# Retention, then a Sinkhorn mixture of experts: X and w1 operands in small steps with moved loads, third tokens after six blocks of columns, Sinkhorn in smaller pieces

## The chip, the core and the metric

The kernel runs on one core of a Trainium2 chip. A time is the device time of one execution in microseconds; the time of a kernel is the median of its runs. The engines are named as in the profile: PE (TensorE), DVE (VectorE), ACT (ScalarE), POOL (GpSimd), SP (SyncE, which issues most DMAs).

## What is computed

```python
# retention: B, H, S, D = 4, 8, 768, 64
for t in range(S):
    state = gamma[None, :, None, None] * state + einsum('bhd,bhe->bhde', k[:, :, t], v[:, :, t])
    y[:, :, t] = scale * einsum('bhd,bhde->bhe', q[:, :, t], state)
x = y.transpose(0, 2, 1, 3).reshape(3072, 512)        # N tokens, D = 512
# mixture of experts: E = 8, F = 1024
P = exp(x @ w_gate - max)                             # (3072, 8)
for _ in range(8):
    P /= P.sum(1, keepdims=True) + 1e-09
    P /= P.sum(0, keepdims=True) + 1e-09
    P *= N / E
for e in range(E):
    out += P[:, e:e + 1] * (maximum(x @ w1[e], 0) @ w2[e])
```

All inputs and the output are float32.

## The kernel before

**Precision and products.** Every float32 operand of the large matmuls is split into a rounded high part (`hi_act`, line 76, on ACT) and the rest (`lo`, line 79: full minus high, on DVE or POOL). A product is then three matmuls: high x high, low x high, high x low. Both large matrix products use a 2 x 2 block scheme with seven products M1 to M7 in place of eight, so operands need sums of blocks ahead (M5, M6, M7, M4 of x; M5, M6, M3, M7 of w1), and results need sums behind.

**Attention stage** (lines 255 to 436). The sequence is cut into 24 chunks (6 places of 128 tokens for each of 4 batches), one chunk `gc` a step `tau` of the loop in line 412. A step decays k on POOL (`tk`), loads the chunk three ahead, splits q and k of the chunk two ahead (`split_qk`: ACT rounds, POOL makes `kl`, DVE makes `QL`), computes the scores of the next chunk (PE, then DVE writes `ta`), the logits of the chunk before, the attention of its own (PE, DVE writes `RX`, SP stores it to `xd` in DRAM) and the state update (PE, DVE adds). Steps 20 to 23 have no state update. SP's queue is in order: the loads of a step stand behind the store of the step before. At the end of step 8 (`tau == 2 * B`) SP is given the load of X0 (the first third of the tokens, in 8 DMAs of 256 KB) and of the w1 blocks 0 and 1 (512 KB each); from step 9 on two tasks of a list are run in each step: 22 for X0 (`x_tasks`), then 3 for each of the two w1 blocks (`w1_tasks`: four additions on POOL and the rounding on ACT, then two subtractions on DVE).

**First matrix product** (lines 707 to 764). A unit is one block of w1's columns (j, 32 of them) by one third of the tokens (r = 0, 1, 2): seven products of 6 matmuls of 128 x 128 x 512, 42 in all. Within a unit's row the products stand in the order `ROW` (M6, M1 of the next unit, M3, M7, M2 and M5 of the next, M4); after each come its results' sums (`post`, `sums`, `last_sum`, on ACT and DVE) and, at certain places m of the row, a task from the list `wq` (w1 blocks) or `xq` (X). Each engine runs its instructions in the order written here. X0 holds the first third, X1 the second; the third goes into X0 again. w1 blocks are converted in jobs, with three buffers `WA` and two raw buffers in `RW`. The list `order` (line 244) gives the units: units 0 to 31 are r = 0 over all 32 blocks; units 32 to 34 are r = 1 of blocks 29, 30, 31; units 35 to 37 are r = 2 of the same; then one block at a time with r = 1 and 2, and the last three blocks as a group. At unit 0 the X1 tasks begin (line 709; its loads stand ahead of the units in SP's queue, with w1 block 2 behind them, line 710); at unit 32 X0 is loaded with the third tokens and its tasks are queued, two after every product (lines 723 to 725, 747).

**Sinkhorn** (lines 450 to 506). The list `sink` has 19 pieces, run one at the end of each unit from 12 to 30: the maximum (DVE reduces, PE transposes, DVE reduces), the exponential (PE broadcasts, then 17 DVE instructions, with XSC as scratch, which the X tasks use too), 8 pairs of row and column steps, and a transposition of P.

**Second matrix product** (lines 533 to 770): units of the same kind over the experts and the three thirds. The change doesn't touch it.

## Time and profile before

| | |
|---|---|
| median of 3 runs | 2055.17 us (2054.22 to 2057.34) |
| profiled execution | 2053.89 us, span 2051.8 us |
| mean granted clock of PE | 0.987 |
| PE, DVE, ACT, POOL busy | 1985.9, 1527.7, 1041.7, 406.0 us |
| DMA | 504.13 MB, mean 246 GB/s |
| attention stage | to 166.3 us |
| first matrix product | 166.3 to 1136.3 us |
| second matrix product | 1136.3 us to the end |

The profile is one execution. Busy time is the sum of an engine's instructions; "idle" in a row is the time before an instruction in which its engine did nothing, with what ended that. The granted clock is the share of full speed that PE was given. A table of windows gives each engine's busy time in a stretch, so stages can be told apart. The chain of work that ended last is by line 42% `L190` (the first product's matmuls) and 25% and 19% `L551` (the second's).

### The profile page before, as it was taken

The page shows a single profiled execution, that of the slowest core. Times are in us where ns is not written, and L with a number is a line of the kernel's source. Part 1 is how long each engine was busy: PE and PEld are TensorE (multiplying, and loading weights), DVE is VectorE, ACT ScalarE, POOL GpSimd, SP SyncE. Part 2 cuts the span into 40 slices and gives each one's busy share as a digit, 9 for nine tenths or more (in the row PEclk, how much of TensorE's full clock was granted, in tenths as well). Part 3 has the DMA queues.
Part 4 walks back from the last instruction along what each step waited for, and adds up shares of the span by engine and source line. Part 5 has one row for each costly group of instructions (what it writes and reads, how often), then busy time and mean ns, then how long its engine had stood idle before and what let it go on. Part 6 is the DMA issues. An engine that isn't in the chain of part 4 may idle for free.

```text
span 2051.8 us, 28824 instructions
## 1 busy us (share of the span) xinstructions
PE 1985.9 (97%) x9273; PEld 1647.2 (80%) x9273; DVE 1527.7 (74%) x2083; ACT 1041.7 (51%) x1668; POOL 406.0 (20%) x422
## 2 busy tenths in 40 slices
PE   7797999998899999999999999999999999999998
PEld 7786887887688888888887788888888888888887
DVE  6795988995666666666677787878778777868766
ACT  3343564554444444444444565655555555655553
POOL 5462342341211121121123000100100101001001
PEclk9899999999999999999999999999999999999999
DMA  7755776776466666666667888998999999999997
GB/s 240 239 180 163 242 245 206 244 244 217 165 233 214 218 228 217 221 218 223 220 229 263 297 286 281 278 288 277 285 283 278 267 291 270 291 292 269 271 269 184
DMA packets 253191, 504.13 MB, mean 246 GB/s; under 512 B 27824, under 2 KB 40432, under 8 KB 250992
## 3 DMA queue, kind: packets, MB, share of 16 engines
q1 hardware_dynamic: 241088, 458.78, 66.3%
q0 software_dynamic: 11952, 43.52, 11.0%
q8 instruction: 72, 1.18, 0.2%
q14 instruction: 79, 0.65, 0.1%
HBM read 269.31 MB, written 232.88 MB: 245 GB/s over the span
## 4 chain that ended last, share of the span: by engine, by line
PE 90%; DVE 4%; DMA 3%; issue 1%; ACT 1%; SPq 1%; POOL 0%; DVEq 0%; ACTq 0%
PE psA L190 42%; PE psA L551 25%; PE psB L551 19%; DMA raw<-kT 1%; DVE QL L80 1%; PE ps_s L327 1%; PE ps_x L363 1%; DMA RW<-w 1%; PE psA L372 1%; PE ps_x L358 0%; PE ps_t L339 0%; DVE X L80 0%; DVE ta L330 0%; SPq L112 0%; DMA hd<-OT 0%
## 5 line engine op out<-in xcount | busy, mean ns | idle before, releaser
L190 PE MATMUL psA<-X,WA 128*128 128x512 f32 x4032 | 931.4, 393 | 24.1 <-DVE OT L213 18.8
L190 PEld LDWEIGHTS psA<-X,WA 128*128 128x128 f32 x4032 | 760.8, 189 | 190.2 <-DVE OT L213 20.9
L77 ACT ACTIVATE WA<-WA 128x512 fp32r<-128x512 f32 x668 | 403.1, 629 | 259.3 <-PE psB L551 116.7
L551 PE MATMUL psA<-WA,X 128*128 128x512 f32 x2296 | 531.4, 389 | 0.2 <-DVE XSC L562 0.2
L551 PEld LDWEIGHTS psA<-WA,X 128*128 128x128 f32 x2296 | 431.0, 188 | 89.9 <-issue 0.6
L551 PE MATMUL psB<-WA,X 128*128 128x512 f32 x1728 | 404.3, 390 | 5.1 <-ACT WA L77 3.1
L80 DVE TENSOR_TENSOR WA<-WA,WA 128x512 fp32r<-128x512 f32 x487 | 313.7, 685 | 99.4 <-ACT WA L77 94.9
L551 PEld LDWEIGHTS psB<-WA,X 128*128 128x128 f32 x1728 | 324.6, 188 | 74.8 <-ACT WA L77 4.2
L158 POOL TENSOR_TENSOR RW<-RW 128x256 f32<-128x256 f32 x244 | 220.8, 915 | 637.9 <-DMA RW<-w 412.8
L219 ACT ACTIVATE OT<-OT 128x512 f32<-128x512 f32 x96 | 60.7, 632 | 243.3 <-DVE OT L218 243.3
L80 DVE TENSOR_TENSOR WA<-RW,WA 128x768 fp32r<-128x768 f32 x122 | 142.5, 1169 | 54.0 <-ACT WA L77 53.9
L569 POOL DMA_DIRECT2D out<-XSC x56 | 48.5, 865 | 611.7 <-DVE XSC L564 365.6
L80 DVE TENSOR_TENSOR WA<-WA 128x512 fp32r<-128x512 f32 x181 | 121.7, 697 | 35.4 <-ACT WA L77 34.4
L213 DVE TENSOR_TENSOR OT<-psA,OT 128x512 f32<-128x512 f32 x96 | 66.2, 689 | 106.2 <-PE psA L190 106.2
L77 ACT ACTIVATE WA<-RW 128x768 fp32r<-128x768 f32 x122 | 109.4, 946 | 23.6 <-POOL RW L158 13.9
L225 DVE TENSOR_TENSOR OT<-psA,OT 128x512 f32<-128x512 f32 x96 | 66.2, 690 | 58.5 <-ACT OT L219 51.3
L229 ACT ACTIVATE OT<-psA 128x512 f32<-128x512 f32 x96 | 57.5, 599 | 77.1 <-PE psA L190 40.3
L236 DVE TENSOR_TENSOR OT<-OT 128x512 f32<-128x512 f32 x96 | 92.2, 961 | 3.3
L579 ACT ACTIVATE OT<-psA 128x512 f32<-128x512 f32 x96 | 57.4, 598 | 72.7 <-PE psA L551 68.8
L226 ACT ACTIVATE OT<-OT 128x512 f32<-128x512 f32 x96 | 60.7, 633 | 65.4 <-DVE OT L225 65.3
L240 DVE TENSOR_TENSOR OT<-OT 128x512 f32<-128x512 f32 x96 | 70.1, 730 | 30.0 <-ACT OT L229 26.1
L211 ACT ACTIVATE OT<-psA 128x512 f32<-128x512 f32 x96 | 57.4, 598 | 64.0 <-PE psA L190 63.9
(116 smaller groups left out, 1486.4 us busy)
## 6 DMA issues: line engine op xcount, KB each, us to landing
hd<-OT SPq DMA_DIRECT2D x672, 256.0 KB, 2.6
WA<-hd SPq DMA_DIRECT2D x668, 256.0 KB, 6.1
RW<-w SPq DMA_DIRECT2D x61, 512.0 KB, 4.5
out<-XSC POOLq DMA_DIRECT2D x56, 512.0 KB, 8.3
RW<-w SPq DMA_DIRECT2D x16, 1024.0 KB, 7.7
out<-OT POOLq DMA_DIRECT2D x27, 512.0 KB, 8.4
OT<-pd SPq DMA_DIRECT2D x23, 512.0 KB, 6.2
raw<-kT SPq DMA_DIRECT2D x24, 256.0 KB, 4.0
```

Source lines behind the costliest of these rows:

```text
L77: act.activation(o, i, AF.Copy)
L80: eng.tensor_tensor(o, full, rd(h), ALU.subtract)
L158: eng_add.tensor_tensor(x[:, WP[o]], x[:, WP[p]], x[:, WP[q]], op)
L190: pe.matmul(ps, w[:, a, k * P:(k + 1) * P], x[:, b, k * 512:(k + 1) * 512], start=i in PRE and k == 0 and m == 0, stop=k == 1 and m == 2, ...
L213: dve.tensor_tensor(c12, ps, u2, ALU.add)
L219: act.activation(o, o, AF.Relu)
L225: dve.tensor_tensor(o, ps, s1, ALU.add)
L226: act.activation(o, o, AF.Relu)
L229: act.activation(self.new("A12"), ps, AF.Relu)
L236: dve.tensor_tensor(t["S2"], t["S1"], t["A11"], ALU.subtract)
L240: dve.tensor_tensor(self.new("S4"), self.t["A12"], self.t["S2"], ALU.subtract)
L551: pe.matmul(ps[d] if isinstance(ps, tuple) else ps[:, d, :], w[:, a, q * 256 + d * P:q * 256 + d * P + P], h[b], start=i in PRE and q == 0 ...
```

## The change

Seven edits:
- `x_load` can load one half of a third of the tokens (one of its two places in the sequence) by itself; M2's loads come second. X0's first half (4 DMAs) is asked for at step 5, its second half at step 8, behind w1 blocks 0 and 1.
- w1 blocks 2 and 3 are loaded at step 16 of the attention stage. Before, block 2 came behind X1's loads and block 3 after unit 0.
- `x_tasks`: 22 steps as before, but the rounding on ACT is issued some steps ahead of the subtraction that reads it, and the sums of blocks stay on DVE.
- `w1_tasks` has four steps: the rounding on ACT is a step of its own. They are run after the products 0, 3, 5, 6 of a unit's row (before: three steps at 0, 1, 5).
- In the attention stage the w1 tasks come first, interleaved, from step 10 on; X0's tasks follow, two a step, and the last two after the logits.
- Order: units 32 to 37 are r = 1 of six blocks, 38 to 40 r = 2 of three of these, 41 to 43 r = 2 of the first three, for which w1 is converted again (64 jobs, before 61). X1's tasks begin at unit 1; the third tokens are loaded at unit 32, and their tasks run from unit 33 on, five a unit, every third subtraction on POOL.
- Sinkhorn has 23 pieces, from unit 14 on: the maximum in three, the exponential in three of six instructions; the transposition is at unit 38.

```diff
--- before.py
+++ after.py
@@ -106,16 +106,16 @@
             q.pop(0)()
 
 
-    def x_load(t, r):
-        for i, c, d in ((M1, 0, 0), (M7, 1, 0), (M3, 1, 1), (M2, 0, 1)):
-            for k in range(2):
+    def x_load(t, r, which=(0, 1)):
+        for i, c, d in ((M1, 0, 0), (M2, 0, 1), (M7, 1, 0), (M3, 1, 1)):
+            for k in range(2) if c in which else ():
                 sp.dma_start(rd(t[:, XP[i], 1, k * 512:(k + 1) * 512]).rearrange("p (b s) -> p b s", s=C),
                              xd[2 * r + c][:, :, 2 * d + k, :])
 
     def x_tasks(t, engs):
+
         q = []
         sc = {M7: 0, M5: 1, M6: 2, M4: 3}
-        e = [engs[k % len(engs)] for k in range(22)]
         for k in range(2):
             def w(i, a=1, k=k):
                 return t[:, XP[i], a, k * 512:(k + 1) * 512]
@@ -123,25 +123,19 @@
             def src(i, w=w):
                 return XSC[:, sc[i], :] if i in sc else rd(w(i))
 
-            def tt(o, a, b, src=src):
-                eng = e.pop()
-                q.append(lambda: eng.tensor_tensor(XSC[:, sc[o], :], a, b, ALU.subtract))
-
-            def one(i, w=w, src=src):
-                eng = e.pop()
-
-                def f():
-                    hi_act(w(i, 0), src(i))
-                    lo(eng, w(i, 1), src(i), w(i, 0))
-                q.append(f)
-
-            b12 = rd(w(M7))
-            tt(M5, b12, src(M1))
-            tt(M6, src(M3), src(M5))
-            tt(M7, src(M3), b12)
-            tt(M4, src(M2), src(M6))
-            for i in (M1, M5, M2, M6, M7, M3, M4):
-                one(i)
+            def step(n, w=w, src=src):
+                b12 = rd(w(M7))
+                hi = [M1, M2, M5, M6, M7, M3, M4][n] if n < 7 else None
+                if n < 4:
+                    o, a, b = [(M5, b12, src(M1)), (M6, src(M3), src(M5)), (M7, src(M3), b12), (M4, src(M2), src(M6))][n]
+                    dve.tensor_tensor(XSC[:, sc[o], :], a, b, ALU.subtract)
+                else:
+                    i = [M1, M5, M2, M6, M7, M3, M4][n - 4]
+                    lo(engs[n % len(engs)], w(i, 1), src(i), w(i, 0))
+                if hi is not None:
+                    hi_act(w(hi, 0), src(hi))
+
+            q += [lambda n=n, step=step: step(n) for n in range(11)]
         return q
 
 
@@ -162,13 +156,15 @@
             tt(M6, M5, M1, ALU.subtract)
             tt(M3, M2, M6, ALU.subtract)
             tt(M7, M1, M7, ALU.subtract)
+
+        def rounded():
             hi_act(a[:, 0:3, 0, :], x[:, 0:3, :])
             hi_act(a[:, 3:7, 0, :], x[:, 3:7, :])
 
         def rest(s):
             lo(eng_lo, a[:, s, 1, :], x[:, s, :], a[:, s, 0, :])
 
-        return [adds, lambda: rest(slice(0, 3)), lambda: rest(slice(3, 7))]
+        return [adds, rounded, lambda: rest(slice(0, 3)), lambda: rest(slice(3, 7))]
 
 
     ps_A = ctx.enter_context(tc.tile_pool(name="ps_A", bufs=1, space=PSUM))
@@ -242,8 +238,11 @@
 
 
     order = [(j, j, 0) for j in range(NJ)]
-    for g in [[NJ - 3, NJ - 2, NJ - 1]] + [[j] for j in range(NJ - 4, 2, -1)] + [[2, 1, 0]]:
-        order += [(j if j >= NJ - 3 else 2 * NJ - 4 - j, j, r) for r in (1, 2) for j in g]
+    order += [(j, j, 1) for j in (NJ - 3, NJ - 2, NJ - 1)]
+    order += [(NJ + k, NJ - 4 - k, r) for r in (1, 2) for k in range(3)]
+    order += [(NJ + 3 + k, NJ - 3 + k, 2) for k in range(3)]
+    for g in [[j] for j in range(NJ - 7, 2, -1)] + [[2, 1, 0]]:
+        order += [(2 * NJ - 1 - j, j, r) for r in (1, 2) for j in g]
     jobs, first, last = {}, {}, {}
     for n, (job, j, r) in enumerate(order):
         jobs[job] = j
@@ -424,13 +423,19 @@
                 attend(tau)
                 for t in late.get(tau, [tau]):
                     hold(t)
+                if tau == B + 1:
+                    x_load(X0, 0, (0,))
                 if tau == 2 * B:
-                    x_load(X0, 0)
                     w1_load(0)
                     w1_load(1)
-                    todo += x_tasks(X0, [dve]) + w1_tasks(0, pool, dve) + w1_tasks(1, pool, dve)
-                if tau > 2 * B:
+                    todo += [f for g in zip(w1_tasks(0, pool, dve), w1_tasks(1, pool, dve)) for f in g]
+                    x_load(X0, 0, (1,))
+                    todo += x_tasks(X0, [dve])
+                if tau > 2 * B + 1:
                     run(todo, 2)
+                if tau == 4 * B:
+                    w1_load(2)
+                    w1_load(3)
             logits(NCHUNK - 1)
             dve.tensor_copy(L.rearrange("p a b -> p (a b)"), PS1[0][:, :NTILE * E])
             run(todo, 20)
@@ -449,32 +454,39 @@
 
         def sink_max():
             dve.tensor_reduce(mx, L.rearrange("p a b -> p (a b)"), AX.X, ALU.max)
+
+        def sink_max2():
             ps = ps_m.tile([P, P], F32, name="pmx", tag="m")
             pe.transpose(ps[:1, :], mx, ident)
             dve.tensor_reduce(mrow[:, 0:1], ps[:1, :], AX.X, ALU.max)
 
-        def sink_exp():
+        def sink_max3():
             ps = ps_m.tile([P, E], F32, name="pmb", tag="m")
             pe.matmul(ps[:, 0:1], ones[:1, :], mrow[:, 0:1], start=True, stop=True)
             dve.tensor_copy(mx, ps[:, 0:1])
+
+        def sink_exp():
             x, n, r, q = [et[:, i, :] for i in range(4)]
             s1, s2 = [ei[:, i, :].bitcast(mybir.dt.int32) for i in range(2)]
...
+            l2, p2 = [t.rearrange("p a b -> p (a b)") for t in (L, Pm)]
+            ops = [
+                lambda: dve.tensor_scalar(x, l2, mx, -104.0, ALU.subtract, ALU.max),
...
+                lambda: dve.tensor_tensor(p2, q, s2.bitcast(F32), ALU.mult),
+            ]
+            return ops
 
         def sink_a():
             dve.tensor_reduce(rs, Pm, AX.X, ALU.add)
@@ -503,7 +515,10 @@
             sp.dma_start(pd[0:P, :], o[:, 0, :])
             sp.dma_start(pd[P:, :], o[:64, 1, :])
 
-        sink = [sink_max, sink_exp] + [sink_a, sink_b] * SINKHORN + [sink_t]
+        sop = sink_exp()
+        sink = [sink_max, sink_max2, sink_max3]
+        sink += [lambda k=k: run(sop, 6) for k in range(3)]
+        sink += [sink_a, sink_b] * SINKHORN + [sink_t]
 
         xt = [X0, X1, X0]
         UA = [UnitA(n, j, r, job, xt[r]) for n, (job, j, r) in enumerate(order)]
@@ -705,14 +720,12 @@
 
 
         x_load(X1, 1)
-        wq = []
-        xq = x_tasks(X1, [dve])
-        w1_load(2)
+        wq, xq = [], []
         loaded = conv = 2
         for i in PRE:
             UA[0].mm(i)
             UA[0].post(i)
-        loaded = 3
+        loaded = 4
         PS2 = None
         carry = None
         for n, u in enumerate(UA):
@@ -720,9 +733,12 @@
             while conv < loaded and n >= first[conv] - 2 and n > last.get(conv - 3, -1):
                 wq += w1_tasks(conv, pool, dve)
                 conv += 1
+            if n == 1:
+                xq = x_tasks(X1, [dve])
             if n == NJ:
                 x_load(X0, 2)
-                xq = x_tasks(X0, [dve, pool])
+            if n == NJ + 1:
+                xq = x_tasks(X0, [dve, dve, pool])
             if n == 40:
                 ps_s.close()
                 ps_B = ctx.enter_context(tc.tile_pool(name="ps_B", bufs=1, space=PSUM, reuse_waits="tile"))
@@ -741,10 +757,10 @@
                     carry.last_sum()
                 if m == 4:
                     u.sums()
-                if m in (0, 1, 5):
+                if m in (0, 3, 5, 6):
                     run(wq, 1)
-                if m in (1, 6) or n >= NJ:
-                    run(xq, 2 if n >= NJ else 1)
+                if m in (1, 6) or n >= NJ and m in (0, 3, 5):
+                    run(xq, 1)
                 for f, x in w2_plan.get((n, m), ()):
                     w2_first(f, x)
                 if n == NUA - 2 and m in (5, 6):
@@ -758,8 +774,10 @@
             while loaded < len(jobs) and loaded <= conv + 1 and n + 1 >= first[loaded] - 3:
                 w1_load(loaded)
                 loaded += 1
-            if 12 <= n < 12 + len(sink):
-                sink[n - 12]()
+            if 14 <= n < 13 + len(sink):
+                sink[n - 14]()
+            if n == 38:
+                sink[-1]()
         carry.last_sum()
         for s in range(12, NHL + 4):
             h_load(s)
```

More of the change, by code (lines that the diff above doesn't have):

```diff
@@ L459, in sink_exp @@
             dve.tensor_copy(mx, ps[:, 0:1])
+        def sink_exp():
             x, n, r, q = [et[:, i, :] for i in range(4)]
             s1, s2 = [ei[:, i, :].bitcast(mybir.dt.int32) for i in range(2)]
-            l2 = L.rearrange("p a b -> p (a b)")
-            dve.tensor_scalar(x, l2, mx, -104.0, ALU.subtract, ALU.max)
-            dve.tensor_scalar(n, x, LOG2E, MAGIC, ALU.mult, ALU.add)
-            dve.tensor_scalar(n, n, MAGIC, None, ALU.subtract)
-            dve.scalar_tensor_tensor(r, n, -LN2_HI, x, ALU.mult, ALU.add)
@@ L467, in sink_exp @@
-            dve.scalar_tensor_tensor(r, n, -LN2_LO, r, ALU.mult, ALU.add)
-            dve.tensor_scalar(x, n, -126.0, None, ALU.max)
-            dve.tensor_tensor(n, n, x, ALU.subtract)
-            dve.tensor_scalar(s1, x, 127.0, 8388608.0, ALU.add, ALU.mult)
-            dve.tensor_scalar(s2, n, 127.0, 8388608.0, ALU.add, ALU.mult)
-            dve.tensor_scalar(q, r, EXPC[0], None, ALU.mult)
-            for c in EXPC[1:]:
-                dve.scalar_tensor_tensor(q, q, c, r, ALU.add, ALU.mult)
@@ L475, in sink_exp @@
-            p2 = Pm.rearrange("p a b -> p (a b)")
-            dve.scalar_tensor_tensor(q, q, 1.0, s1.bitcast(F32), ALU.add, ALU.mult)
-            dve.tensor_tensor(p2, q, s2.bitcast(F32), ALU.mult)
+            l2, p2 = [t.rearrange("p a b -> p (a b)") for t in (L, Pm)]
+            ops = [
+                lambda: dve.tensor_scalar(x, l2, mx, -104.0, ALU.subtract, ALU.max),
+                lambda: dve.tensor_scalar(n, x, LOG2E, MAGIC, ALU.mult, ALU.add),
+                lambda: dve.tensor_scalar(n, n, MAGIC, None, ALU.subtract),
+                lambda: dve.scalar_tensor_tensor(r, n, -LN2_HI, x, ALU.mult, ALU.add),
+                lambda: dve.scalar_tensor_tensor(r, n, -LN2_LO, r, ALU.mult, ALU.add),
+                lambda: dve.tensor_scalar(x, n, -126.0, None, ALU.max),
+                lambda: dve.tensor_tensor(n, n, x, ALU.subtract),
+                lambda: dve.tensor_scalar(s1, x, 127.0, 8388608.0, ALU.add, ALU.mult),
+                lambda: dve.tensor_scalar(s2, n, 127.0, 8388608.0, ALU.add, ALU.mult),
+                lambda: dve.tensor_scalar(q, r, EXPC[0], None, ALU.mult),
+            ]
@@ L479, in sink_a @@
+            ops += [lambda c=c: dve.scalar_tensor_tensor(q, q, c, r, ALU.add, ALU.mult) for c in EXPC[1:]]
+            ops += [
+                lambda: dve.scalar_tensor_tensor(q, q, 1.0, s1.bitcast(F32), ALU.add, ALU.mult),
+                lambda: dve.tensor_tensor(p2, q, s2.bitcast(F32), ALU.mult),
+            ]
+            return ops
         def sink_a():
```

## The prediction

> **What bounds the kernel now.** I read the page's busy times first, then the table of windows with one row per stage, then TensorE's waits, and last the timeline at each place where TensorE stands still.
>
> ```profile
> span 2051.8 us, 28824 instructions
> PE 1985.9 (97%) x9273; PEld 1647.2 (80%) x9273; DVE 1527.7 (74%) x2083; ACT 1041.7 (51%) x1668; POOL 406.0 (20%) x422
> ```
>
> TensorE is busy for 97% of the span, so nothing that merely shortens another engine's work can show; only TensorE's stops, and its time at a lower clock, can be won back. Where these are:
>
> ```profile
> 42.00:64.00 22.00, 21.98 (x214) 20.83 (x215) 19.88 (x32) 8.01 (x14) 13.52 (x14) 1.00 0.74 243
> 64.00:76.00 12.00, 10.09 (x100) 9.31 (x98) 6.53 (x10) 0.90 (x2) 3.16 (x3) 1.00 0.91 271
> 76.00:96.00 20.00, 11.63 (x70) 11.10 (x70) 11.56 (x18) 7.63 (x13) 8.67 (x7) 0.57 0.63 217
> 96.00:131.00 35.00, 31.47 (x302) 29.07 (x303) 34.40 (x51) 15.17 (x26) 23.05 (x18) 1.00 0.64 206
> 131.00:138.00 7.00, 7.00 (x42) 6.45 (x41) 5.28 (x10) 2.11 (x5) 2.24 (x3) 0.52 0.53 152
> 166.28:222.25 55.97, 47.75 (x193) 37.72 (x193) 35.21 (x43) 24.00 (x39) 19.02 (x20) 0.94 0.65 207
> 222.25:345.34 123.09, 117.89 (x503) 95.43 (x504) 108.33 (x148) 66.49 (x106) 43.88 (x48) 0.97 0.70 228
> 345.34:490.39 145.05, 145.05 (x650) 119.89 (x648) 127.06 (x195) 76.62 (x118) 47.62 (x52) 1.00 0.71 238
> 490.39:537.53 47.14, 34.70 (x136) 26.64 (x133) 27.77 (x33) 19.03 (x36) 16.05 (x11) 0.89 0.52 165
> 537.53:1109.47 571.94, 571.94 (x2520) 472.56 (x2520) 368.98 (x482) 267.88 (x425) 110.65 (x122) 1.00 0.64 222
> 1136.30:2051.80 915.50, 909.29 (x4008) 752.26 (x4008) 711.62 (x985) 518.02 (x830) 71.74 (x83) 1.00 0.92 275
> ```
>
> TensorE's waits, as engine and tile, what it waited for, total us, times, longest:
>
> ```profile
> PE psA L190 <- DVE OT L213: 18.8, 5, 5.9
> PE ps_s L327 <- DVE ta L330: 15.2, 7, 10.3
> ...
> PE pmx L453 <- DVE mx L451: 2.2, 1, 2.2
> ```
>
> The columns after a window's length are PE, weight load, DVE, ACT and POOL busy (with counts), granted clock, DMA share and GB/s. The row from 537.53 has no stop in 2520 matmuls: 571.94 / 2520 = 0.227 us each, 9.53 us for a unit of 42. Measured against that, the three windows with a clock under 1.00 lose: 193 matmuls from 166.28 should take 43.8 us and take 55.97 (12.2 lost, units 0 to 3); from 222.25, 503 less the five small ones of the Sinkhorn part are 498, 113.0 us against 123.09 (10.1 lost); from 490.39, 136 less the two transposes are 134, 30.4 us against 47.14 (16.7 lost). Together 39.0 us. The last row, the second matrix product, is at full clock and not touched. The attention stage before 166.28 is the fourth place: TensorE waited 10.3 us at a time for DVE's `ta`, and 20 us of it ran at a granted clock of 0.57, 7 us at 0.52.
>
> **Start of the units (12.2 us lost).** The timeline:
>
> ```profile
> 171.86 2.23 SPq L152 DMA_DIRECT2D RW<-w  x1
> ...
> 178.79 0.84 ACT L77 ACTIVATE WA<-RW 128x768 fp32r<-128x768 f32 x1 [6.14 <-DMA RW<-w]
> 178.84 4.05 POOL L158 TENSOR_TENSOR RW<-RW 128x256 f32<-128x256 f32 x4 [22.49 <-DMA RW<-w]
> 179.66 1.51 DVE L80 TENSOR_TENSOR WA<-RW,WA 128x768 fp32r<-128x768 f32 x1 [9.58 <-ACT WA L77]
> ```
>
> w1 block 2 is asked for at 171.86, behind the eight loads of X1 on SP; ACT waits 6.14 us for it, DVE 9.58 us for ACT, and unit 0's sums queue behind that. Block 3 repeats it one unit later. The change loads both blocks in the attention stage, so ACT's and DVE's waits lose their cause. What is late next: POOL's four additions (4.05 us) start as soon as POOL is free, and ACT's rounding comes three products later (a product is 6 matmuls, 1.36 us), so it finds them done; X1 (2 MB) is wanted one unit later than before. Block 4 is asked for after unit 0, a whole unit before its additions. Two subtractions (M3, M4 of X0) are left for after the logits copy, 2 x 0.69 us on DVE, beside the first 18 matmuls (4.1 us). I leave 1.2 us of the 12.2: gain 11.0 (9 to 12).
>
> **Sinkhorn (10.1 us lost).**
>
> ```profile
> 320.36 0.32 DVE L463 TENSOR_SCALAR XSC<-L,mx 128x192 f32<-128x192 f32 x1
> ...
> 326.00 0.78 DVE L477 TENSOR_TENSOR Pm<-XSC 128x192 f32<-128x192 f32 x1
> ```
>
> The 17 instructions of the exponential occupy DVE from 320.36 to 326.78, 6.4 us in one piece, and one of the five L213 waits above follows; the transpose waited 2.2 us for the maximum issued right before it. Now the 17 come in three pieces (about 2.1 us each) at three units' ends, and transpose and broadcast come a unit after what they read. The row from 345.34 prices such pieces: there each unit has one Sinkhorn step (rows, or columns with a small matmul), and 15 units take 145.05 / 15 = 9.67 us each, 0.14 over. So six units with pieces cost 0.8, say 1.0, and I leave as much for the X1 operands ahead of them: 2.0 stays, gain 8.1. If DVE (108.33 of 123.09 us busy) can't hold 2.1 us more in a unit, it is 5.
>
> **Third tokens (16.7 us lost).**
>
> ```profile
> 501.27 5.38 SPq L112 DMA_DIRECT2D X<-xd  x8
> ...
> 508.65 0.69 DVE L128 TENSOR_TENSOR XSC<-X,XSC 128x512 f32<-128x512 f32 x1 [7.10 <-DMA X<-xd]
> ```
>
> X0 is loaded over from 501.27 and its 22 tasks are issued at once, two at every product: DVE stands 7.10 us in front of data with the units' sums behind, then runs 22 tasks in less than two units. Now the tasks begin a unit later (509.6 on this clock; what DVE waited for had come at 508.65), five to a unit, and the third tokens are first read in unit 37's row instead of unit 34's. The rounding is issued ahead of its subtraction, so DVE no longer waits for ACT. Is there room on DVE? Prices:
>
> ```profile
> L80 DVE TENSOR_TENSOR WA<-RW,WA 128x1024 fp32r<-128x1024 f32 x28 | 41.5, 1483 | 0.0
> ...
> L80 DVE TENSOR_TENSOR WA<-RW,WA 128x768 fp32r<-128x768 f32 x27 | 26.3, 973 | 5.5 <-ACT WA L77 5.5
> ```
>
> Mean ns stand behind the bar. A w1 block costs DVE 1.48 + 0.97 = 2.46 us. From 537.53, 60 units with a block in every second take 368.98 / 60 = 6.15, so the sums alone are 6.15 - 1.23 = 4.9. Units 33, 34 and 35 each convert a block (jobs 32 to 34) beside X0's tasks: 4.9 + 2.46 + 5 x 0.69 = 10.8 us for two of them, 9.4 for the one with two subtractions on POOL, 7 and less after. Two units are 1.3 over 9.53, and the products give DVE about two of their slots (2.7 us) before a bank is wanted again. I leave 2.2 us: gain 14.5 (8 to 16). The three additional w1 blocks (units 41 to 43) need 7.4 us of DVE in a 9.53 us unit, and their 4 us of POOL and 512 KB lie in rows where POOL is 19% busy: nothing, and 1 to 2 us if a block came late.
>
> **Attention stage (0, between -7 and +8).** Its loop takes one chunk a step, and five moves touch it, with both signs. First, between two chunks' loads SP issued 3 MB (eight X loads, two w1 loads), and the 10.3 us wait follows; now it is 2 MB there, 6.9 by proportion: 3.4 gained. Second, the other MB is three steps earlier; the same price is 3.4, but the row from 42 has the DMA engines 26% idle, 5.7 us of 22: I take 1.0 lost. Third, POOL now gets both blocks' eight additions in one step, where a step is about 5.3 us:
>
> ```profile
> 141.13 1.40 DVE L80 TENSOR_TENSOR QL<-raw,QH 64x512 fp32r<-64x512 f32 x2
> ...
> 144.86 4.14 POOL L158 TENSOR_TENSOR RW<-RW 128x256 f32<-128x256 f32 x4
> ...
> 147.21 2.35 DVE L80 TENSOR_TENSOR QL<-raw,QH 64x512 fp32r<-64x512 f32 x2
> ```
>
> That is 8.3 us, and `tk` of the next step, which TensorE's state update reads, and `kl` queue behind. POOL is otherwise 13.52 / 22 busy, so some 2 us a step are free, and they come while TensorE recovers from the wait above: 1.5 lost, 0 to 4. The same rows show a price to DVE: its pair of subtractions took 2.35 us beside the additions, 1.40 without. The Trainium skill ("SBUF — State Buffer", Who interferes with whom) says that a DVE instruction with two SBUF inputs and a GpSimd instruction that reads SBUF exclude each other for the whole of the one that came first; the trace agrees in direction with +0.95 us a pair, and the rule, which speaks against this edit, would add about 1 us for the longer burst.
> Fourth, X0's 22 tasks move from steps 9 to 19 to steps 14 to 23, w1's subtractions from the end to steps 12 and 13. DVE is the bound where the tasks lie (34.40 of 35.00 us) but not before (19.88 of 22.00). It is the same work; formerly four tasks lay in the wait, now eight lie in the last four steps, where chunks have no state update: 0, plus or minus 2. Fifth, 1 MB of w1 at step 16 delays that chunk's loads by up to 3.4; the DMA share is 0.64 there: 1.0 lost. Sum: 3.4 - 1.0 - 1.5 - 1.0 = -0.1, taken as 0. The ends: with the second, third and fifth at their dear ends (3.4 + 4 + 3.4) and 3.4 gained it is +7.4, with 0.6 for the tasks +8; the clock makes the other. The stretches at half cost 11.63 - 70 x 0.103 = 4.4 and 7.00 - 42 x 0.103 = 2.7 us beyond the waits (0.103 = 22.00 / 214 from the first row); half of that may go with the shorter wait, so -7 with the 3.4. At 131 the clock fell after a stretch in which TensorE was 31.47 of 35.00 us busy, so gaps far shorter than 10 us can cost a half-rate stretch. The Trainium skill ("TensorE: Matmul & The Clock Gate", What's actually happening) has the clock halve after one idle window of about 3.4 us; the stretch at 131 speaks against that as a lower limit, and by the rule alone the waits that I price at 1.0 and 1.5 would leave the clock at full.
>
> **Sum.** 11.0 + 8.1 + 14.5 + 0 = 33.6 us. The profiled execution took 2053.89 us (span 2051.8 and 2.1 around it), 1.3 below the median of the three runs: 2053.9 - 33.6 = 2020.3, and 2021.6 as a median.
>
> **Rivals.** (1) DVE becomes the bound in units 33 to 37: if its real lag there is twice what I left room for, a stop at each of the five units and one half-rate stretch keep about 9 of the 16.7: 2028 to 2030. For it speaks that DVE was 88% busy where X tasks and w1 blocks met with the Sinkhorn pieces (108.33 of 123.09 us); against it that five are issued per unit, not fourteen. Chance 0.14. (2) Splitting the burst only makes two waits of one: the stage loses 8 by two gaps with a half-rate stretch each, 2030. For it: at 64 to 76 DMA is at 0.91, so a MB costs its full time; against it: the idle 26% before. Chance 0.11. (3) Slower: the clock stays at half through the attention stage. At 0.52, 42 matmuls took 7.00 us, 0.167 each, against 0.103: a 5.3 us step becomes 8.5, 3.2 more. With gaps in steps 7, 10, 12, 13 and 17 it could hold over the 16 steps 7 to 22; about three are at half already. It turns the sign from 11 more steps on (33.6 / 3.2 = 10.5); all 13 more give 2021.6 + 41.6 = 2063. Against it: full clock came back by 96 and 138 each time. Chance 0.04. (4) The change doesn't do what it says for the third tokens: not DVE's wait but the eight loads on SP, with the units' stores behind them, set the stop. Then 16.7 stays less 2: 2034. For it: 5.38 us of issue ahead of the stores; against it: DVE's 7.10 us is on the data itself. Chance 0.04.
>
> **The numbers.** Forecast 0.67, rivals 0.14, 0.11, 0.04 and 0.04. The forecast's own ends: 2021.6 - 7 in the attention stage - 3 in what I left elsewhere = 2011; up, the rivals (1) and (2), both together 2036. I give 2010 to 2037. What a measurement can tell from no change is 0.2%, about 4 us: all cases but (3) are faster by more. Faster 0.94, within 0.02, slower 0.04.
>
> **What would show it.** Right: in the profile after, units 0 to 3 and 12 to 15 at 9.5 to 9.9 us, no L213 wait over 1 us, no unit of 32 to 40 above 11 us, clock 1.00 from 166 on, units starting near 166 as now. Wrong: a wait for DMA `RW<-w` or `X<-xd` left in DVE's or ACT's rows after 166; POOL `tk` as releaser of TensorE near 85; the first unit starting over 8 us later or earlier; DVE near 100% from unit 33 to 36.

## The result, and the profile after

The changed kernel takes 2042.4 us (median of 11 runs, 2037.2 to 2053.0) against 2055.9 us (11 runs): a ratio of 0.9934, 95% interval 0.9917 to 0.9951. It is faster by 13.6 us; the forecast was a gain of 33.6. Its profiled execution took 2037.68 us, 16.2 below the one of before (2053.89) and at the low end of its own runs, so the two profiles show a little more gain than the medians.

The page of the changed kernel:

```profile
span 2035.6 us, 28904 instructions
PE 1986.9 (98%) x9273; PEld 1646.5 (81%) x9273; DVE 1547.5 (76%) x2096; ACT 1039.3 (51%) x1674; POOL 432.2 (21%) x427
```

TensorE has the same 9273 instructions; DVE and POOL are 20 and 26 us busier. I cut both profiles at the first matmul of the units and at units 4, 12, 16, 32, 41 and 94. First the kernel before, then the changed one (the columns are those of the first table of windows):

```profile
166.28:220.42 54.14, 46.23 (x187) 36.77 (x188) 33.38 (x42) 23.34 (x37) 17.34 (x19) 0.94 0.64 203
220.42:298.00 77.58, 77.17 (x338) 62.56 (x337) 71.13 (x88) 46.26 (x75) 30.91 (x34) 1.00 0.75 246
298.00:345.34 47.34, 42.24 (x174) 33.81 (x173) 39.03 (x62) 20.88 (x32) 14.65 (x17) 0.93 0.62 201
345.34:500.04 154.70, 154.70 (x692) 127.86 (x691) 131.71 (x202) 80.60 (x126) 47.62 (x52) 1.00 0.71 235
500.04:603.04 103.00, 90.56 (x380) 72.78 (x379) 63.84 (x80) 44.62 (x74) 26.12 (x23) 0.95 0.58 197
603.04:1107.95 504.91, 504.91 (x2228) 417.50 (x2226) 326.72 (x426) 236.78 (x375) 100.33 (x110) 1.00 0.64 222
```

```profile
171.21:216.03 44.82, 44.49 (x187) 36.04 (x187) 31.88 (x41) 23.94 (x39) 9.96 (x12) 0.96 0.71 223
216.03:294.10 78.07, 77.72 (x337) 62.52 (x336) 74.99 (x90) 44.31 (x73) 33.64 (x32) 1.00 0.73 243
294.10:333.03 38.93, 38.73 (x171) 31.18 (x169) 34.60 (x40) 20.82 (x34) 17.51 (x16) 1.00 0.76 244
333.03:491.23 158.20, 157.39 (x689) 126.94 (x687) 142.40 (x206) 78.02 (x125) 58.92 (x55) 1.00 0.69 230
491.23:586.66 95.43, 89.72 (x387) 72.37 (x386) 74.47 (x110) 47.29 (x80) 28.53 (x27) 0.98 0.71 228
586.66:1091.76 505.10, 505.10 (x2227) 417.55 (x2226) 326.53 (x430) 235.48 (x378) 108.00 (x112) 1.00 0.65 223
```

Row by row: the units begin 4.9 us later (171.21 against 166.28); units 0 to 3 gain 9.3, 4 to 11 lose 0.5, 12 to 15 (Sinkhorn's start before) gain 8.4, **16 to 31 lose 3.5**, 32 to 40 gain 7.6, the rest is equal. Together 16.2. The gains came where they were forecast, at the third tokens (units 32 to 40) half as large; three places, the attention stage, units 4 to 11 and units 16 to 31, gave some of it back.

What the attention stage looks like now, TensorE's timeline at three of its gaps:

```profile
62.88 0.55 PE L326 MATMUL ps_s<-QH,kh 128*128 128x256 f32 x1 [4.28 <-DVE ta L329]
...
88.59 0.55 PE L326 MATMUL ps_s<-QH,kh 128*128 128x256 f32 x1 [5.24 <-DVE ta L329]
...
116.84 0.55 PE L326 MATMUL ps_s<-QH,kh 128*128 128x256 f32 x1 [2.42 <-ACT QH L77]
```

Instead of one wait of 10.3 us there are two, of 4.3 and 5.2, one behind each part of X0's load. The windows show the granted clock (third column from the end) after each:

```profile
42.00:61.94 19.94, 16.17 (x156) 15.14 (x156) 14.01 (x21) 5.97 (x11) 10.28 (x10) 1.00 0.79 258
61.94:72.18 10.24, 9.30 (x49) 8.78 (x50) 6.06 (x11) 2.92 (x5) 5.12 (x5) 0.50 0.40 129
72.18:85.83 13.65, 11.17 (x109) 10.39 (x107) 5.93 (x10) 1.77 (x3) 3.77 (x5) 1.00 1.02 324
85.83:96.07 10.24, 7.48 (x40) 7.29 (x42) 7.63 (x11) 6.05 (x9) 9.93 (x11) 0.50 0.41 136
96.07:116.55 20.48, 17.65 (x172) 16.25 (x168) 19.22 (x24) 6.81 (x12) 14.52 (x13) 1.00 0.63 206
116.55:119.97 3.42, 3.13 (x15) 3.16 (x16) 3.34 (x7) 1.34 (x3) 0.98 (x1) 0.50 0.37 93
```

Each wait is followed by 10.2 us at half (the half-rate stretch begins within the wait), and a gap of 2.42 us by 3.4.

### The profile page after: what moved, and what is told of

Its sections match the earlier page's. It is cut to its first block, busy times and chain, and to the rows that moved or that the text cites. A ratio compares the mean times of both kernels' runs of the same rounds, so it can differ in the third digit from the quotient of the medians.

```text
span 2035.6 us, 28904 instructions
## 1 busy us (share of the span) xinstructions
PE 1986.9 (98%) x9273; PEld 1646.5 (81%) x9273; DVE 1547.5 (76%) x2096; ACT 1039.3 (51%) x1674; POOL 432.2 (21%) x427
## 3 DMA queue, kind: packets, MB, share of 16 engines
q0 software_dynamic: 11952, 43.52, 11.1%
## 4 chain that ended last, share of the span: by engine, by line
PE 89%; DVE 4%; DMA 3%; issue 1%; ACT 1%; SPq 1%; POOL 0%; DVEq 0%; ACTq 0%
PE psA L186 42%; PE psA L566 26%; PE psB L566 19%; DMA raw<-kT 1%; DVE QL L80 1%; DVE WA L80 1%; PE ps_s L326 1%; DMA hd<-OT 1%; DVE OT L230 1%; PE ps_x L362 1%; PE ps_x L357 0%; DMA raw<-qT 0%; PE psA L371 0%; SPq L283 0%; DVE ta L329 0%
## 5 line engine op out<-in xcount | busy, mean ns | idle before, releaser
L80 DVE TENSOR_TENSOR WA<-WA,WA 128x512 fp32r<-128x512 f32 x487 | 314.0, 685 | 99.9 <-ACT WA L77 95.4
L152 POOL TENSOR_TENSOR RW<-RW 128x256 f32<-128x256 f32 x256 | 256.3, 1011 | 628.0 <-DMA RW<-w 395.6
L215 ACT ACTIVATE OT<-OT 128x512 f32<-128x512 f32 x96 | 60.7, 632 | 287.1 <-DVE OT L214 287.1
L209 DVE TENSOR_TENSOR OT<-psA,OT 128x512 f32<-128x512 f32 x96 | 66.2, 690 | 146.4 <-PE psA L186 145.8
L80 DVE TENSOR_TENSOR WA<-RW,WA 128x768 fp32r<-128x768 f32 (+1 forms) x128 | 166.4, 1338 | 0.1
L80 DVE TENSOR_TENSOR WA<-WA 128x512 fp32r<-128x512 f32 x181 | 121.8, 698 | 35.1 <-ACT WA L77 28.1
L77 ACT ACTIVATE WA<-RW 128x768 fp32r<-128x768 f32 (+1 forms) x128 | 114.0, 938 | 3.0 <-POOL RW L152 3.0
L236 DVE TENSOR_TENSOR OT<-OT 128x512 f32<-128x512 f32 x96 | 72.1, 751 | 21.4 <-ACT OT L225 21.1
L230 DVE SCALAR_TENSOR_TENSOR OT<-OT 128x512 f32<-128x512 f32 x96 | 79.6, 829 | 0.7
```

What stands on the lines that cost most here:

```text
L77: act.activation(o, i, AF.Copy)
L80: eng.tensor_tensor(o, full, rd(h), ALU.subtract)
L152: eng_add.tensor_tensor(x[:, WP[o]], x[:, WP[p]], x[:, WP[q]], op)
L209: dve.tensor_tensor(c12, ps, u2, ALU.add)
L215: act.activation(o, o, AF.Relu)
L230: dve.scalar_tensor_tensor(t["S1"], TMP[:, 3, :], 0.0, t["A22"], ALU.max, ALU.add)
```

## The experiments

All start from the changed kernel unless said otherwise. Each set was timed beside the kernel before (2053.4 to 2054.5 us). The stage times are from each run's own profile: "from step 7" is the time from the first logits matmul of step 7 to that of the last chunk, units by the first matmul of their row. A unit of pure matmuls is 9.52 us, nine are 85.7, sixteen with one Sinkhorn matmul in every second 154.7.

| kernel | us | ratio to before (95%) | steps 7 to 11 | from step 7 | units 16-31 | units 32-40 |
|---|---|---|---|---|---|---|
| before | | 1 | 41.4 | 110.7 | 154.7 | 103.0 |
| changed | 2042.4 | 0.9934 (0.9917-0.9951) | 44.3 | 115.2 | 158.2 | 95.4 |
| e1 X0 load whole | 2037.1 | 0.9926 (0.9906-0.9946) | 40.2 | 112.5 | 158.0 | 95.4 |
| e2 Sinkhorn pauses | 2038.5 | 0.9930 (0.9910-0.9951) | 44.2 | 114.9 | 158.9 | 92.2 |
| e3 no POOL for X0 | 2038.9 | 0.9928 (0.9911-0.9944) | 43.3 | 115.3 | 158.4 | 94.3 |
| e4 w1 places | 2035.8 | 0.9909 (0.9888-0.9931) | 40.6 | 111.3 | 154.8 | 94.2 |
| e5 one load a step | 2036.8 | 0.9918 (0.9900-0.9935) | 34.4 | 112.6 | 158.5 | 95.2 |
| e6 w1 2, 3 late | 2036.8 | 0.9919 (0.9903-0.9935) | 40.0 | 110.7 | 158.5 | 95.0 |
| e7 units 33-37 lightened | 2036.7 | 0.9920 (0.9900-0.9941) | 40.5 | 111.3 | 158.8 | 90.0 |
| e8 e4, e5, e7 together | 2023.1 | 0.9852 (0.9830-0.9874) | 32.9 | 108.8 | 154.7 | 89.2 |
| e9 rounding early | 2040.8 | 0.9946 (0.9930-0.9963) | 41.9 | 114.8 | 156.7 | 95.3 |
| e10 e5, additions apart | 2037.1 | 0.9917 (0.9896-0.9938) | 29.5 | 113.0 | 158.6 | 95.0 |
| e11 e8, additions apart | 2020.8 | 0.9834 (0.9818-0.9850) | 31.6 | 112.9 | 154.6 | 90.7 |
| e12 before, order alone | 2042.2 | 0.9944 (0.9929-0.9959) | 40.6 | 110.5 | 154.6 | 91.7 |
| e13 reload spread | 2038.7 | 0.9924 (0.9902-0.9946) | 41.5 | 111.1 | 158.7 | 93.4 |
| e14 e11 and e13 | 2019.2 | 0.9836 (0.9814-0.9857) | 29.9 | 105.1 | 154.8 | 87.8 |
| e15 tasks after the stage | 2049.0 (one run) | | 43.2 | 103.2 | | |
| e16 e15, one load a step | 2035.5 (one run) | | 31.4 | 94.3 | | |

The single edits' medians overlap; it is the stage times that tell them apart. The changed kernel, e2, e3, e4, e7, e9 and e13 have the same attention stage instruction by instruction: 111.1 to 115.3 from step 7 on, mean 113.4, so a difference of one profile under 4 us there says nothing. Units 16 to 31 repeat better: 158.0 to 158.9 in the nine timed kernels with the changed kernel's w1 places.

**e1, the split of X0's load.**

```diff
-                if tau == B + 1:
-                    x_load(X0, 0, (0,))
...
-                    x_load(X0, 0, (1,))
+                    x_load(X0, 0)
```

> The changed kernel, but all eight X0 loads are asked for at step 8, behind w1 blocks 0 and 1, none at step 5. Theory (each load burst costs its own wait of DVE plus a half-rate stretch of TensorE): steps 7 and 8, which now take 11.1 and 8.4 us, fall back to 5.3 each (9 us less), step 10 grows from 12.0 to 16 to 18; the units start near 167, some 4 us earlier than the 171.2 of the changed kernel, and the time is about 2 to 4 us less. Rival (the w1 blocks' additions and subtractions in steps 10 to 13 make the stage longer, the split costs nothing): the units start at 171 or later.

Steps 7 and 8 took 5.3 each, step 10 16.3, and the units started at 168.5. The theory's places were right. What the split costs in all is not settled: steps 7 to 11 take 40.2 with the whole load, 40.5 to 44.3 (mean 42.3) in the seven profiles with the split, and 40.0 in e6, which has the same instructions up to step 11. The 2.4 us that the prediction had the split win are in none of these profiles; that it loses any is not shown.

**e5 and e10, one load a step, and POOL's additions.** e5 puts the loads at steps 5 and 7 (w1 0, 1), 8 to 15 (one X0 load each), 16 and 18; e10 also issues the additions of block 0 in step 8 and those of block 1 in step 9:

```diff
-                if tau > 2 * B + 1:
+                if tau in (2 * B, 2 * B + 1):
+                    run(todo, 1)
+                if tau > 2 * B + 2:
                     run(todo, 2)
```

> The changed kernel, but no step asks for more than one extra load: w1 block 0 at step 5, block 1 at step 7, the eight X0 loads one a step from 8 to 15, w1 blocks 2 and 3 at steps 16 and 18. The tasks stay where they are. Theory (the stage is long because bursts of 1 to 2 MB keep the next chunk's k and q from arriving; 256 to 512 KB fit into the DMA engines' idle quarter): steps 7, 8, 10 and 11, in the changed kernel 11.0, 8.4, 12.0 and 7.6 us, come to 5.3 to 6.5 each, 14 to 17 us less, the units start near 156, the time is 12 to 16 us less than the changed kernel's. Rival (POOL's eight additions in step 10 and the order of the tasks hold steps 10 and 11): these two stay above 8 us, the gain is 8 or less.

> The run with one load a step, but POOL's additions of w1 block 0 are issued in step 8 and those of block 1 in step 9, not all eight in step 10. In that run step 11 took 9.6 us and TensorE once waited 2.7 us for POOL's tk. If eight additions in a row are the cause, step 11 comes to 5.3 to 6.5 us and steps 9 and 10 stay under 7: 3 to 4 us less in the stage. If not, step 11 stays above 8.

Both theories held where they pointed, but not in the time: e5's units started at 173.4, not near 156, and its median is 6 us under the changed kernel's, not 12 to 16. e5: steps 7 to 10 at 7.0, 5.3, 7.2 and 5.3; step 11 at 9.6, in which TensorE waited for POOL:

```profile
PE ps_t L338 <- POOL tk L305: 2.7, 1, 2.7
```

With the additions apart that wait is gone and step 11 takes 5.4. Steps 7 to 11 fell from 44.3 to 34.4 to 29.5. But the whole from step 7 did not: 115.2, 112.6, 113.0. Steps 12 to 23 grew from 70.8 to 78.2 to 83.5. e10's windows of these steps, and those of the changed kernel:

```profile
87.20:170.80 83.60, 70.86 (x571) 64.74 (x569) 69.36 (x94) 26.29 (x44) 41.54 (x33) 0.84 0.52 171
```

```profile
98.85:169.70 70.85, 63.29 (x570) 58.48 (x569) 65.95 (x93) 24.40 (x41) 38.68 (x33) 0.93 0.54 175
```

DVE's work is nearly the same (69.4 and 66.0 us); it is 93% busy in the second. In e10 the clock stood at 0.84 there. e14, further down, has the same instructions as e10 in these steps and took 75.2:

```profile
83.60:158.80 75.20, 64.13 (x570) 58.79 (x568) 69.17 (x94) 25.54 (x43) 42.24 (x33) 0.93 0.57 186
```

**e15 and e16, loads without tasks.** The 30 tasks run after the logits, w1 blocks 2 and 3 are loaded after them, so the units start late.

> The changed kernel with all loads of the attention stage up to step 8 in place, but none of the 30 tasks run in it: they come after the logits, and w1 blocks 2 and 3 are loaded after them (the output is the same, the units start later). It shows what the loads alone cost: if the two bursts are it, steps 7, 8, 10 and 11 keep some 16 to 18 us over 5.3 each and all later steps up to 21 fall to 5.3 or less; if the tasks are, steps 10 and 11 get short too.

> The same with one load a step (w1 at steps 5 and 7, X0 from 8 to 15): neither bursts nor tasks. If bursts and DVE's tasks are all that lengthens the stage, every step from 5 to 21 takes 5.3 to 5.6 us and the logits end near 140 to 145; what stays above that has a cause of its own.

e15 has steps 7, 8, 10 and 11 at 10.8, 8.5, 13.2 and 5.4, and 12 to 23 at 60.0: the bursts make the first three long, the tasks step 11; e16 has 31.4 and 62.9, with most steps at 5.3 and some at 6.4 to 7.2, and the last logits at 150.8, not 140 to 145. So, by one profile each, the bursts alone are 43.2 - 31.4 = 11.8 us of steps 7 to 11, the tasks alone 70.8 - 60.0 = 10.8 of steps 12 to 23. What e5 and e10 save on the first they lost again in the second; e14, with the same instructions as e10, lost 4 of the 14 (29.9 and 75.2, against 44.3 and 70.8). What sets this is open; see below.

**e6, w1 blocks 2 and 3 at step 16 or after the stage.**

```diff
-                if tau == 4 * B:
-                    w1_load(2)
-                    w1_load(3)
...
+        w1_load(2)
+        w1_load(3)
         x_load(X1, 1)
```

> The changed kernel, but w1 blocks 2 and 3 are not loaded at step 16 of the attention stage but right ahead of X1's loads, as the first DMAs after the stage. If the megabyte at step 16 costs what the prediction said (1.0 us, up to 3.4), steps 17 and 18, now 8.3 and 7.8 us, get shorter by that, and the units start 1 to 3 us earlier. If those two steps have another cause (they were 7.8 and 8.1 in the kernel before, without the loads), the start stays at 171 within 1 us. Units 0 to 3 (44.8 us) take 1 us more at most either way, because the blocks now arrive before X1.

Steps 17 and 18 took 8.0 and 7.9 without the loads (8.3 and 7.8 with them, 7.8 and 8.1 before), so the megabyte at step 16 costs nothing that shows. And units 0 to 3 took 44.7 us as in the changed kernel: to stand ahead of X1's loads, not behind them, was enough to end the wait of before. The earlier start (166.6) lies in steps 7 to 11 (40.0 against 44.3), where the two kernels have the same instructions.

**e4 and e9, the places of the w1 steps.** `if m in (0, 3, 5, 6)` becomes `(0, 1, 3, 5)` in e4 and `(0, 1, 5, 6)` in e9.

> The changed kernel, but the four w1 steps stand after products 0, 1, 3 and 5 of a unit's row instead of 0, 3, 5 and 6. Theory (both subtractions at the row's end, 2.5 us, pile up with the sums and the Sinkhorn piece in front of M3's sum; ACT's rounding in mid-row delays M4's copy): units 16 to 31, 158.2 us in the changed kernel and 154.7 in the kernel before, lose 2 to 3.5 us. Rival (these units are longer because more Sinkhorn and w1 work is in them at all): no change within 1 us.

> The changed kernel, with the w1 steps after products 0, 1, 5 and 6: against the run with 0, 1, 3 and 5 only the subtractions are back at the row's end, the rounding stays early. If the pile of both subtractions at the row's end made units 16 to 31 longer, they stay at 157 to 158 us (158.2 in the changed kernel, 154.8 with 0, 1, 3, 5); if it was ACT's rounding in mid-row, they come to 154.7 to 155.5.

Units 16 to 31 in e4:

```profile
328.20:483.00 154.80, 154.80 (x689) 127.57 (x688) 135.14 (x205) 80.71 (x125) 61.71 (x54) 1.00 0.71 235
```

154.8: all 3.4 us are back, and TensorE has no stop in the stretch, with the same Sinkhorn pieces in it. Units 4 to 15 gain 2.7 more (114.3 against 117.0). e9 lies between, 156.7: the rounding in mid-row accounts for 1.5, the pile of subtractions for 1.9. The pile, in DVE's timeline of the changed kernel at the end of a unit:

```profile
363.54 2.62 DVE L80 TENSOR_TENSOR WA<-RW,WA 128x768 fp32r<-128x768 f32 x2
...
366.08 0.34 DVE L479 TENSOR_TENSOR XSC<-XSC 128x192 f32<-128x192 f32 x1
...
367.64 0.69 DVE L236 TENSOR_TENSOR OT<-OT 128x512 f32<-128x512 f32 x1
368.24 0.68 DVE L209 TENSOR_TENSOR OT<-psA,OT 128x512 f32<-128x512 f32 x1
```

Both subtractions (L80), a Sinkhorn piece (from L479) and L236, the last sum of the unit before, stand in one run, without a pause, in front of L209, the sum that frees M3's bank.

**e2, e3, e7, e12, e13: units 32 to 40.**

```diff
# e2: last Sinkhorn pieces after unit 37
+        sink_at = list(range(14, 33)) + [38, 39, 40, 43]
# e3
-                xq = x_tasks(X0, [dve, dve, pool])
+                xq = x_tasks(X0, [dve])
# e7: e2, e3, and four X steps in units 33 to 35
-                if m in (1, 6) or n >= NJ and m in (0, 3, 5):
+                if m in (1, 6) or n >= NJ and m in ((0, 3) if n < 36 else (0, 3, 5)):
```

> The changed kernel, but the last three Sinkhorn pieces wait while the third tokens are converted: pieces at units 14 to 32, then 38 to 40, the transposition at 43 (the last PSUM pool opens at 46). Theory (in units 33 to 36 DVE is over its limit because Sinkhorn steps of 1.6 to 2 us, a w1 block and five X steps fall into one unit): units 32 to 40 lose 3 to 5 us of their 9.7, unit 34 falls from 16.2 to 11 to 12 us; time 3 to 5 us less. Rival (POOL's work beside DVE's is what makes DVE late): under 1.5 us less.

> The changed kernel, but all of the third tokens' subtractions are on DVE, none on POOL. Rival of the run before (POOL's two-input work stretches DVE's instructions, which took 1.2 to 1.75 us instead of 0.69 from 512 to 521): units 32 to 40 get 2 to 4 us shorter although DVE has four instructions more. Theory (DVE is simply given too much in these units): four more instructions of 0.69 are 2.8 us more of DVE, units 32 to 40 get 1 to 3 us longer.

> The changed kernel, with the three loads on DVE in units 33 to 37 lightened together: last Sinkhorn pieces after unit 37, no subtraction on POOL, four X steps a unit (not five) in units 33 to 35 and five in 36 and 37. Theory (DVE's sum of work in these units decides): each of units 33 to 35 has 4.9 + 2.5 + 4 x 0.69 = 10.1 us of DVE against 11 to 13 now, so units 32 to 40, 95.4 us in the changed kernel, come to 87 to 90; time 5 to 8 us less. Rival (the reload of X0 itself, 2 MB ahead of w1 block 33 and of the units' stores, holds unit 34): unit 34 stays above 12 us.

e2 gains 3.2 in units 32 to 40, as forecast, though row 34 falls only to 14.9, not to 11 to 12; it gives 2.3 back in units 41 to 43, where the moved pieces meet w1 blocks. e3 gains 1.1 with four instructions more on DVE: neither side of that pair is right, what POOL's four subtractions (of 14) cost DVE is a little more than what they spare it. e7 gains 5.4, row 34 falls from 16.2 to 11.2, rows 36 to 38 to 9.5 to 9.7; row 35 rises from 9.7 to 11.1. So e2 and e7 show that DVE has too much work in these rows. How it looks, in the changed kernel's row 34:

```profile
511.96 4.98 POOL L152 TENSOR_TENSOR RW<-RW 128x256 f32<-128x256 f32 x4 [11.28 <-DMA RW<-w]
512.04 1.48 DVE L80 TENSOR_TENSOR WA<-RW,WA 128x768 fp32r<-128x768 f32 x1
...
513.44 1.23 DVE L131 TENSOR_TENSOR XSC<-X,XSC 128x512 f32<-128x512 f32 x1
...
514.59 1.75 DVE L80 TENSOR_TENSOR WA<-RW,WA 128x1024 fp32r<-128x1024 f32 x1
...
516.27 1.22 DVE L80 TENSOR_TENSOR X<-X 128x512 fp32r<-128x512 f32 x1
...
516.89 3.08 POOL L80 TENSOR_TENSOR X<-XSC,X 128x512 fp32r<-128x512 f32 x2
...
517.83 1.02 DVE L503 SCALAR_TENSOR_TENSOR Pm<-Pm,ct 128x192 f32<-128x192 f32 x1
518.77 1.75 DVE L236 TENSOR_TENSOR OT<-OT 128x512 f32<-128x512 f32 x1
...
522.31 14.11 PE L186 MATMUL psA<-X,WA 128*128 128x512 f32 x54 [3.21 <-DVE OT L209]
```

POOL is at work all along, and DVE's instructions with two inputs in SBUF are longer than the prediction had them: X's steps take 1.22 us and a sum 1.75 where it put 0.69, the w1 pieces 1.48 and 1.75 where it put 0.97 and 1.48, and a Sinkhorn instruction of 0.36 takes 1.02. The Trainium skill ("SBUF — State Buffer", Who interferes with whom) has such an instruction wait for the whole of a GpSimd instruction that reads SBUF; in this row the trace agrees, with an addition on POOL of about 1.25 us (4.98 / 4) and some 0.3 to 1.1 us more on each of DVE's.

Then row 34 kept its stop in a kernel where there was no Sinkhorn piece left:

> The kernel before, with the new order of units, the new X steps and their places alone; loads, w1 steps, attention stage and Sinkhorn (units 12 to 30, so it is over before the third tokens come) as before. If Sinkhorn's late pieces are what units 33 to 36 can't hold in the changed kernel, units 32 to 40 take 90 to 93 us here (103.0 before, 95.4 after); if X steps with w1 blocks on DVE and POOL alone are too much, 94 or more. Time 10 to 13 us less than before in the first case, 8 or less in the second.

e12 (the kernel before with the new `order`, the new `x_tasks` and their places alone) takes 91.7 us for units 32 to 40 and is 11.7 us under the kernel before (2053.9 beside it), the first case of what was expected. Its ratio, 0.9944 (0.9929 to 0.9959), can't be told from that of all seven edits, 0.9934 (0.9917 to 0.9951): by the two profiles the others win 18 us in units 0 to 3 and 12 to 15 and lose 9 in the other units up to 40, but little of that shows in the medians. In e12 all rows of units 32 to 40 are at 9.5 but row 34, which takes 15.5. The timeline has two rows that the theory of DVE's load doesn't explain, SP's and DVE's:

```profile
504.97 6.71 SPq L112 DMA_DIRECT2D X<-xd  x8
511.78 5.24 SPq L194 DMA_DIRECT2D hd<-OT  x7
```

```profile
521.92 0.69 DVE L219 TENSOR_TENSOR OT<-psA,OT 128x512 f32<-128x512 f32 x1 [1.95 <-DMA hd<-OT]
```

The units' stores stand behind the eight loads, and DVE waits for a result's buffer whose store has not landed. That is the prediction's fourth rival. The wait is 1.95 of the 6.0 us that the row loses; behind it DVE again works beside POOL, at 1.2 to 2.05 us an instruction. In the changed kernel the same sum waits too, at the end of row 33:

```profile
510.10 0.69 DVE L221 TENSOR_TENSOR OT<-psA,OT 128x512 f32<-128x512 f32 x1 [2.26 <-ACT X L77]
```

The profile names an instruction of ACT that writes another tile; a store asked for at 503.17 landed 6.8 us later, just ahead of 510.10, and in e13 this wait is gone. e13 puts one load after each product of row 32:

```diff
-            if n == NJ:
-                x_load(X0, 2)
...
+                if n == NJ:
+                    for i, c, d, kk in [(M1, 0, 0, 0), (M7, 1, 0, 0), (M3, 1, 1, 0), (M2, 0, 1, 0),
+                                        (M1, 0, 0, 1), (M7, 1, 0, 1), (M3, 1, 1, 1), (M2, 0, 1, 1)][m:m + 1 if m < 6 else 8]:
+                        sp.dma_start(rd(X0[:, XP[i], 1, kk * 512:(kk + 1) * 512]).rearrange("p (b s) -> p b s", s=C),
+                                     xd[4 + c][:, :, 2 * d + kk, :])
                 if m == 0 and carry is not None:
```

> The changed kernel, but the eight loads that put the third tokens into X0 are not asked for in one go ahead of unit 32: one stands after each product of row 32 (two after the last), so the units' stores lie between them on SP. Fourth rival of the prediction (the stores queue behind the reload, and a result's buffer is not free when DVE wants it; in the run with the order alone DVE's L219 waits 1.95 us for DMA hd<-OT in row 34): row 34, 16.2 us in the changed kernel, comes to 10 to 13, units 32 to 40 lose 3 to 5 us. Theory so far (DVE's load alone): row 34 stays above 14.

Row 34 falls from 16.2 to 10.1; row 35 takes 12.8 (9.7 before that), so units 32 to 40 gain 2.0 us, where 3 to 5 were forecast: with the stores out of the way DVE's load shows one row later. Both causes are real and stand one behind the other.

**e8, e11, e14: together.**

> All that the theories ask for together: loads one a step, w1 steps after products 0, 1, 3 and 5, and the lightened units 33 to 37. If the causes are separate the gains add: 14 us in the attention stage, 6 in units 4 to 31, 6 in units 32 to 40: 2015 to 2020 us. If they share a bound (DVE has the same work in all), a third or more is missing: above 2024.

> The version with everything together and the additions apart. If the additions cost the stage 3 to 4 us there too (step 11 took 9.0 us), the median is 2018 to 2021 against 2023; if DVE's work in steps 12 to 21 takes the gain back, it stays at 2022 to 2024.

> The version with everything together, additions apart, and the reload spread over row 32. If the reload ahead of the stores is what rows 34 and 35 still lose there (23.5 us for two units of 9.5), they come to 20 us or less and the median to 2016 to 2019, against 2021. If not, 2020 to 2022.

The gains add: by the medians e4, e5 and e7 are 6.6, 5.6 and 5.7 us under the changed kernel, 18 together, and e8, at 2023.1, is 19 under it. By the ratios it is 5, 3 and 3 against 17, with intervals of some 4 us each way, so more than addition is not shown. Its 2015 to 2020 was not reached, and the attention stage is where it fell short (108.8 from step 7 on, 6 gained of 14). e11 and e14 are at 2020.8 and 2019.2; their ratios, 0.9834 and 0.9836, do not differ, nor do they clearly from e8's 0.9852; so which of the forecasts for e11 and e14 holds can't be told from the times. e14's units 32 to 40 take 87.8, and rows 34 and 35 20.2 where 20 was forecast. e14 has the lowest median here: 1.6% below the kernel before, 1.0% below the changed one.

## Why the prediction was wrong

By the two profiles the forecast gain of 33.6 became 16.2; the 17.4 between them are these, each a term of the prediction's sum or one that it lacks:

**Third tokens: forecast 14.5, measured 7.6.** The step that failed is "4.9 + 2.46 + 5 x 0.69 = 10.8 us for two of them". It left Sinkhorn out: with 23 pieces from unit 14 on, the last fall into units 33 to 35, and the edit that moved them was costed only at its own place (e2: 3.2 us). It took 0.69 us for DVE's instructions, measured without POOL beside it, although the prediction itself showed a pair at 2.35 beside POOL and 1.40 without. And the fourth rival, given 0.04, is true in part: the stores stood behind the reload (e12, e13), worth 2.0 us in e13 and 2.9 in e14 against e11, not the 14.7 that the rival kept. "What is late next" was asked for the start of the units, not here; that DVE's 7.10 us wait for the data in the kernel before hid a wait for the stores is likely, but no run tests it. The first rival (DVE becomes the bound, given 0.14) described the result, with its place and nearly its size: it kept about 9 of the 16.7 us, and units 32 to 40 kept 9.7 over 85.7.

**Units 16 to 31: forecast nothing, measured 3.5 lost.** The w1 steps' places were described and never priced. It is the edit without a term in the sum; e4 and e9 show it, 1.9 us the pile of subtractions, 1.5 the late rounding.

**Attention stage: forecast 0, measured 4.9 later in this profile**, 2.8 in the mean of seven (113.4 against 110.7 and, in e12, 110.5). The step that failed is the second: the megabyte at step 5 was taken at 1.0 because the DMA engines were 26% idle, and it cost 5.7 us in step 7 and 3.1 in step 8 (4.7 to 8.8 together in the profiles with the split, nothing in e1). A mean idle share didn't take the burst: SP issues the four loads in 2.7 us ahead of the next chunk's, and that chunk's k, asked for at 51.60, lands 6.3 us later; in e1, without the burst, it is asked for at 48.50 and lands after 4.7 (a step earlier the two profiles agree within 0.1 us). The first term came out larger than its 3.4: step 10 fell from 17.0 to 12.0. The third (POOL's eight additions) was right in kind, 2.7 us of waiting for `tk` in e5; the changed kernel has no wait of TensorE for POOL there. The fifth was priced at 1.0 and costs nothing measurable (e6). The second rival, given 0.11, had the mechanism, two waits made of one with a half-rate stretch each; its 8 us were more than was lost. Rivals 1 and 2 together, which is what came, were put at 2036, inside the range; the median lies 6 us above.

**Start of the units: forecast 11.0, measured 8.8** (units 0 to 11). The mechanism held: no wait for `RW<-w` is left in front of the sums. The forecast was for units 0 to 3, which gained 9.3. The clock was at half for the first 3.4 us, and units 2 to 11 take 0.3 us more each than 9.52, with DVE 74.99 of 78.07 us busy in units 4 to 11.

**Sinkhorn: forecast 8.1, measured 8.4** in units 12 to 15. Right in mechanism and size there; its last pieces are part of what units 33 to 35 lost.

The last 2.6 us, from 16.2 to 13.6, are the profiled execution's place among its kernel's runs: the changed kernel scatters by 16 us, and the prediction's range had no term for it.

Open is why steps 12 to 23 take 75 us in one profile and 83 in another with the same instructions (e14, e10). The half-rate stretches go with it, 10.2 us of these steps in e14 and 26.6 in e10. If TensorE set the pace throughout, the 16.4 us more would cost half, 8.2 by this estimate, and that is the size of the difference; 5.2 of it lies in steps 22 and 23, which are at half clock in e10 (6.5 us each against 3.9). In front of that stretch TensorE waited 1.6 us for DVE's `QL` in e10, and as long in e5 and e11, which have the stretch too; in e14 and e8, which don't, 1.0 and 1.4. Whether the clock makes DVE late or DVE's lateness slows the clock was not separated.

## What to carry to other kernels

When a change moves a piece of work, price it at the place where it lands, together with all that lands there, with durations measured beside the neighbour that will run there. A burst of loads delays what stands behind it in its queue, whatever the mean idle share, and that goes for stores too, whose buffers somebody is waiting for. Where two causes stand one behind the other, taking one away moves the stop: e13 took 6 us off row 34, and 2 off units 32 to 40. And price every place that an edit touches: the new places of the w1 steps, which had no term, lost 3.5 us, and the order of units with the new X steps alone (e12) came within the noise of all seven edits.

## What the runs showed of the hardware

A stop of 2.42 us was enough for a stretch at half clock (the row at 116.84 and the window from 116.55), one of 4 to 5 us was followed by three such stretches of 3.4. The Trainium skill ("TensorE: Matmul & The Clock Gate", What's actually happening) asks for an idle window of about 3.4 us; here a shorter stop did, behind a stretch in which TensorE was 86% busy (17.65 of 20.48 us). Other short stops did not: in the kernel before, 2.22 us at 309.89 and 2.55 us at 521.70 were followed by full clock, so the length of one stop doesn't decide it alone.

The same instructions took 105.1, 112.9 and 113.0 us in the attention stage of e14, e11 and e10, from step 7 on. A single profile of this stage can be 8 us off, more than most of the edits tried here are worth.
